# Gate taps of a causal convolution as 64x64 instead of 32x32 array tiles, with weights in plain channel order and new engine orders

## The chip, the cores and the metric

One core of a Trainium2 chip. The metric is the device time of one execution in microseconds, without the host. A profiled execution also gives a span (from the first to the last instruction that counts), which is about 2 us shorter than its time. Medians are given with the number of runs. Every run is put beside runs of the kernel before on the same chip. The sets of experiments ran on different chips (6, then 5, 4 and 0, in the order below), so where kernels of two sets are compared the text says so: such a difference holds that of the chips and sets too (the kernel before had medians of 246.38, 245.32, 247.37 and 245.95 us there).

## The reference, cut to what matters

Feature-map attention (exp of a projection and of its negative, each shifted by its absolute maximum), then a gated linear unit whose gate is a causal convolution over 5 tokens, one weight per channel and tap. Eight batches, 8 heads x 64 channels, 576 tokens.

```python
proj = einsum('bhsd,df->bhsf', x, w_phi)          # q and k
proj = proj - max(abs(proj)); phi = concat(exp(proj), exp(-proj))
kv, z = einsum(k_p, v), sum(k_p);  x = (q_p @ kv) / (q_p @ z + 1e-6)
...
for k in range(5):
    gate_pre += conv_w[k][None, None, :] * xp[:, k:k + S, :]
out = (sigmoid(gate_pre) * (x @ w_val)) @ w_out
```

## The kernel before

Every step is an entry ("op") with a number. Five fixed tables give the order of the entries on TensorE (PE), VectorE (DVE), ScalarE (ACT), GpSimd (POOL) and the load and store queue (SP); a planner walks them, places PSUM banks and sets the semaphore waits. All batches run through one unrolled program, so nothing is a loop on the chip.

Tokens are split by parity: even tokens in partitions 0 to 63 of a head, odd in 64 to 127. The gate is done on TensorE, as a product with diagonal matrices (`DG`), one per tap:

```python
for a in range(2):                     # two halves of the channel tiles
    gps = [Banks(2, "GATE"), Banks(2, "GATE")]
    for y in range(3):
        steps = (((0, 0),), ((0, 1), (2, 0), (2, 1), (4, 0), (4, 1)), ((1, 0), (1, 1), (3, 0), (3, 1)))[y]
        for k, z in steps:             # tap k, half z of the 64 channels
            for g in range(4):
                for par in range(2):
                    p0, dl = D * par + 32 * z, k // 2 + (k & 1) * (1 - par)
                    matmul(PS[32 * g:32 * g + 32, gps[z].at + (par ^ (k & 1)), 0:HALF],
                           DG[p0:p0 + 32, 2 * g + a, k, :], XT[p0:p0 + 32, 2 * g + a, dl:dl + HALF], ...)
        # the third group (odd taps) waits for the end of the second
    ... tanh (ACT), value projection (PE), product (DVE), two channel tiles a half
```

An odd tap takes a token to the other parity, so its result goes to the other parity's bank. The fence, a wait of one gate group for the end of another, keeps the two row halves of the array out of one bank. The 32-channel tiles need the channels of w_val and w_out in another order: four DVE copies (`WVp`) at the start and four transfers for w_out.

## Time and profile before

| | before |
|---|---|
| time, first set | 248.2 us (248.1 to 249.18, 3 runs) |
| profiled execution | 244.11 us, span 242.3 us |
| TensorE records | 4,624 weight loads, as many matmuls |
| gate | 1,280 of these matmuls and 1,280 loads |

The page gives for each engine how much of 40 equal slices it was busy, in tenths; the granted clock of TensorE and the DMA share stand below in the same slices.

```profile
PE   0587588779897997988789959987789999999960
...
PEclk9999997999999999999979999999999999999997
DMA  5999999955589969699996997996744102210361
```

TensorE has dents in the middle (a 5 in slice 24), and none in slices 31 to 38. The clock's dent in slice 21 follows one pause. The instructions of the gate's line, and what the engine idled for ahead of them:

```profile
L881 PEld LDWEIGHTS PS<-XT,DG x1280: 87/88/92, 51.9 to 226.4; 32*32 32x32 bf16 x183
L881 PE MATMUL PS<-XT,DG x1280: 277/289/293, 51.9 to 226.5; 32*32 32x288 bf16 x183
...
  issue: 10.7, 11
  PE PS L881: 3.7, 14
```

(min/median/max ns; then the idle time in us and how often, by what ended it.) "issue" is the largest, and the 3.7 us in 14 times are the fence. Almost two thirds of the idle time ahead of these instructions (10.7 of 16.8 us over all releasers) has no visible cause. The view counts loads and matmuls as two engines, so a pause of both stands in it twice: of the 10.7 us, 4.2 are the matmuls' own, in two pauses.

### The profile page before, as it was taken

How to read it: one execution, taken by the hardware profiler on the slowest of the kernel's cores; microseconds unless marked ns; L12 is line 12 of the kernel's file. 1: busy time of each engine (PE TensorE's matmuls, PEld its weight loads, DVE VectorE, ACT ScalarE, POOL GpSimd, SP SyncE). 2: the span in 40 equal slices, each digit the busy share in tenths (PEclk: the TensorE clock that was granted, in tenths of full speed). 3: DMA queues.
4: the chain of work that ended last, by engine and by line, in shares of the span. 5: the costliest groups of instructions: out<-in, count | busy, mean ns of one | idle time of the engine just before them, and what ended most of it. 6: DMA issues, size and time to landing. Idle time of an engine off the chain costs nothing.

```text
span 242.3 us, 10298 instructions
## 1 busy us (share of the span) xinstructions
PE 197.7 (82%) x4609; PEld 136.8 (56%) x4624; DVE 178.6 (74%) x286; ACT 177.7 (73%) x253; POOL 125.6 (52%) x213
## 2 busy tenths in 40 slices
PE   0587588779897997988789959987789999999960
PEld 0355356656656784655576546664566767775520
DVE  3399978869999996883859549997779877567520
ACT  3278998899899887796927949997859768742220
POOL 7968599792669794338083982670557610000000
PEclk9999997999999999999979999999999999999997
DMA  5999999955589969699996997996744102210361
GB/s 131 208 212 276 206 228 215 222 65 104 131 211 209 227 142 153 128 225 259 173 222 118 187 177 209 201 153 209 213 88 145 49 3 89 98 40 16 119 219 41
DMA packets 59741, 38.30 MB, mean 158 GB/s; under 512 B 37869, under 2 KB 51565, under 8 KB 59634
## 3 DMA queue, kind: packets, MB, share of 16 engines
q1 hardware_dynamic: 48248, 27.67, 48.5%
q0 software_dynamic: 11280, 9.91, 26.9%
q8 instruction: 36, 0.59, 1.0%
q10 hardware_dynamic: 170, 0.08, 0.1%
q14 instruction: 7, 0.06, 0.1%
HBM read 30.48 MB, written 16.52 MB: 194 GB/s over the span
## 4 chain that ended last, share of the span: by engine, by line
PE 61%; DVE 15%; ACT 8%; issue 6%; DMA 5%; POOL 1%; POOLq 0%; DVEq 0%; SPq 0%
PE PS L901 14%; PE PS L930 10%; PE PS L881 8%; PE PS L794 6%; PE PS L756 5%; DVE MQb L674 3%; DMA QT<-R 3%; PE PS L575 3%; ACT KTIL L586 3%; DVE MK L581 2%; DMA KTIL<-in_q_dram 2%; PE PS L661 2%; PE PS L702 2%; DVE XN L808 2%; ACT QTIL L715 2%
## 5 line engine op out<-in xcount | busy, mean ns | idle before, releaser
L623 POOL TENSOR_TENSOR VT<-VN,EK 128x512 bf16<-128x512 f32 x64 | 65.8, 1046 | 29.4 <-ACT EK L614 17.2
L586 ACT ACTIVATE KTIL<-PS 128x1024 bf16<-128x1024 f32 x64 | 63.0, 1045 | 15.2 <-PE PS L575 14.9
L715 ACT ACTIVATE QTIL<-PS 128x1024 bf16<-128x1024 f32 x64 | 62.1, 1048 | 5.1 <-PE PS L708 4.3
L674 DVE TENSOR_REDUCE MQb<-PS 128x8 bf16<-128x1024 f32 (+1 forms) x40 | 43.8, 1112 | 10.0 <-PE PS L661 9.6
L581 DVE TENSOR_REDUCE MK<-PS 128x8 f32<-128x1024 f32 x32 | 38.7, 1217 | 2.3 <-PE PS L575 1.2
L901 PE MATMUL PS<-XT,WV 64*128 64x288 bf16 x512 | 36.1, 283 | 1.3 <-ACT GS L895 0.5
L907 DVE SCALAR_TENSOR_TENSOR GV<-GS,PS 128x576 bf16<-128x576 bf16 x32 | 23.9, 751 | 15.7 <-PE PS L901 11.8
L895 ACT ACTIVATE GS<-PS 128x576 bf16<-128x576 f32 x32 | 19.2, 649 | 18.9 <-PE PS L881 18.9
L930 PE MATMUL PS<-WO,GV 128*128 128x512 bf16 x113 | 28.7, 380 | 1.8 <-issue 1.0
L901 PEld LDWEIGHTS PS<-XT,WV 64*128 64x128 bf16 x512 | 23.3, 94 | 9.4 <-ACT GS L895 1.4
L881 PE MATMUL PS<-XT,DG 32*32 32x288 bf16 x1280 | 20.5, 287 | 6.0 <-issue 4.2
L794 PE MATMUL PS<-KVSB,QTIL 128*128 128x65 bf16 x512 | 21.3, 198 | 3.6 <-issue 3.2
L756 PE MATMUL PS<-VT,KTIL 128*128 128x65 bf16 x512 | 21.0, 196 | 3.0 <-issue 2.4
L794 PEld LDWEIGHTS PS<-KVSB,QTIL 128*128 128x128 bf16 x512 | 18.6, 100 | 7.1 <-issue 3.7
L808 DVE TENSOR_TENSOR XN<-PS,RC 128x512 bf16<-128x512 f32 x32 | 21.9, 689 | 0.9
L552 ACT ACTIVATE OS<-PS 128x512 f32<-128x512 f32 x26 | 15.6, 611 | 9.3 <-PE PS L930 6.2
L756 PEld LDWEIGHTS PS<-VT,KTIL 128*128 128x128 bf16 x512 | 19.0, 99 | 4.8 <-issue 3.4
L633 POOL TENSOR_TENSOR VTt<-VNt,EK 128x512 bf16<-128x512 f32 x16 | 16.6, 1041 | 8.9 <-ACT EK L614 8.8
L611 POOL TENSOR_SCALAR MK<-MK 128x16 f32<-128x16 f32 (+1 forms) x24 | 5.8, 244 | 27.5 <-DVE MK L581 23.0
L881 PEld LDWEIGHTS PS<-XT,DG 32*32 32x32 bf16 x1280 | 10.8, 88 | 14.2 <-issue 6.5
L930 PEld LDWEIGHTS PS<-WO,GV 128*128 128x128 bf16 x128 | 10.7, 98 | 12.0 <-ACT OS L552 0.7
L575 PE MATMUL PS<-W,KT 64*128 64x128 bf16 x256 | 14.0, 242 | 3.4 <-ACT EK L614 0.9
(85 smaller groups left out, 290.4 us busy)
## 6 DMA issues: line engine op xcount, KB each, us to landing
VN<-in_v_dram SPq DMA_DIRECT2D x16, 512.0 KB, 6.3
out_dram<-OS SPq DMA_DIRECT2D x32, 256.0 KB, 3.3
R<-in_k_dram POOLq DMA_DIRECT2D x12, 288.0 KB, 7.0
R<-in_q_dram POOLq DMA_DIRECT2D x12, 288.0 KB, 5.9
QTIL<-in_k_dram SPq DMA_DIRECT2D x2, 512.0 KB, 5.0
VNt<-in_v_dram SPq DMA_DIRECT2D x32, 32.0 KB, 4.6
out_dram<-OS SPq DMA_DIRECT2D x16, 64.0 KB, 2.4
KTIL<-in_q_dram POOLq DMA_DIRECT2D x2, 256.0 KB, 6.0
```

The lines of the kernel that those rows point to most:

```text
L581: pl.op("Kmax", "DVE", dve(1024), lambda E, at, u=u: [E.tensor_reduce(MK[:, 0, 8 * u:8 * u + 8].rearrange("p (t x) -> p t x", t=2), m.PS[: ...
L586: pl.op("Kexp", "ACT", act(1024), lambda E, at, u=u, g=g: [E.activation(KTIL[:, g, u, :, :, :], m.PS[:, at:at + 2, :].rearrange("p t (x f) ...
L623: pl.op("VT", "POOL", pool(512), lambda E, at, u=u, hh=hh, a=a, g=g, EK=EK: [E.tensor_tensor(m.VT[s][:, g, u, :, :, 0:D], m.VN[s][:, 4 * h ...
L674: pl.op("Qmax", "DVE", dve(256 * nx), lambda E, at, u=u, nx=nx: [E.tensor_reduce(MQb[:, :].rearrange("p (t s) -> p t s", t=2)[:, :, 4 * u: ...
L715: pl.op("Qexp", "ACT", act(1024), lambda E, at, u=u, g=g: [E.activation(m.QTIL[s][:, g, u, :, :, :], m.PS[:, at:at + 2, :].rearrange("p t ...
L756: res.append(E.matmul(m.PS[:, at + sg, x * E1:(x + 1) * E1], m.KTIL[s][:, sg, 2 * g + a, par, x, :], m.VT[s][:, sg, 2 * g + a, par, x, :], ...
L794: return [E.matmul(m.PS[:, at + g, x * E1:(x + 1) * E1], m.QTIL[s][:, sg, 2 * j + g, par, x, :], m.KVSB[s][:, g, sg, x, :], start=(sg == 0 ...
L808: pl.op("NRM", "DVE", dve(512), lambda E, at, view=view, RC=RC, XN=XN, par=par: [E.tensor_tensor(XN[:, :, par, :].rearrange("p (g x) d -> ...
L881: res.append(E.matmul(m.PS[32 * g:32 * g + 32, gps[z].at + (par ^ (k & 1)), 0:HALF], m.DG[p0:p0 + 32, 2 * g + a, k, :], XT[p0:p0 + 32, 2 * ...
L901: return [E.matmul(m.PS[:, at + p, 0:HALF], m.WV[ROWS[p], h, P * jt:P * jt + P], XT[ROWS[p], h, PAD:PAD + HALF], start=(h == 0), stop=(h = ...
L907: pl.op("GV", "DVE", dve(576), lambda E, at, jt=jt, GS=GS: [E.scalar_tensor_tensor(out=m.GV[jt][:, s, :, :], in0=GS[:, :, :], scalar=1.0, ...
L930: return [E.matmul(m.PS[:, at, :], m.GV[jt][:, s, p, P * j:P * j + P], m.WO[:, jt, :], start=(jt == 0), stop=(jt == 3)) for jt in range(4)]
```

## The change

Its intent: the same gate with fewer and larger matmuls, 64 channels of one parity by 64 outputs, so 40 per half instead of 80; channels in plain order, so no weight copies; four groups in two phases (even taps, then odd taps), so that a fenced group follows not on the group it waits for but on the one after. All five order tables are new, made with a model that knows about instruction pages and about the delay before loads start.

```diff
-            for y in range(3):
-                steps = (((0, 0),), ((0, 1), (2, 0), ...), ((1, 0), (1, 1), (3, 0), (3, 1)))[y]
+            for n in range(4):
+                y, ks = n % 2, ((0, 2, 4), (1, 3))[n // 2]
                 def mm(E, at, jt=2 * a + y, ks=ks):
+                    for k in ks:
+                        for hh in range(2):
                             for par in range(2):
+                                h, dl = 2 * jt + hh, k // 2 + (k & 1) * (1 - par)
-                                    m.PS[32 * g:32 * g + 32, gps[z].at + (par ^ (k & 1)), 0:HALF],
-                                    m.DG[p0:p0 + 32, 2 * g + a, k, :], XT[p0:p0 + 32, ...],
+                                    m.PS[ROWS[hh], at + (par ^ (k & 1)), 0:HALF], m.DG[ROWS[par], h, k, :],
+                                    XT[ROWS[par], h, dl:dl + HALF], ...
-   sync=gate[-1:] if y == 2 else []          # third group waits for the second
+   sync=gate[-2:-1] if n > 1 else []         # group 3 waits for 1, group 4 for 2
...
-    for jt in range(4):  pl.op("WVp", "DVE", ...)          # four weight copies
-    const("WO", "POOL", 2.2, ... for g in range(4) ...)    # four transfers
+    const("WO", "POOL", 0.8, ... one transfer ...)
-        pl.op("DG", "POOL", pool(5 * 32), ...)
+        pl.op("DG", ("POOL", "DVE"), ... 5 * D ...)
+LAG = dict(xk=1.9, xt=1.9)
 ORDER = dict(PE=..., DVE=..., ACT=..., POOL=..., SP=...)   # all new
 LATE = {...}                                               # release times of loads, all new
```

## The prediction

> **What bounds the kernel now.** I read the page first, then the busy time of each engine in stretches that I chose (the startup, two middle stretches with TensorE stalls and without, the last stretch), then the chain of waits in order of time, then the timeline at the pauses that the chain shows.
>
> ```profile
> span 242.3 us, 10298 instructions
> PE 197.7 (82%) x4609; PEld 136.8 (56%) x4624; DVE 178.6 (74%) x286; ACT 177.7 (73%) x253; POOL 125.6 (52%) x213
> ...
> 12.00:52.00 40.00, 30.69 (x526) 21.67 (x529) 34.98 (x57) 35.00 (x50) 31.80 (x55) 0.96 1.17 216
> 52.00:94.00 42.00, 38.30 (x1048) 27.34 (x1048) 38.28 (x54) 37.60 (x55) 30.28 (x52) 1.00 0.79 163
> 94.00:142.00 48.00, 38.85 (x923) 26.94 (x928) 32.39 (x50) 35.58 (x54) 25.13 (x44) 0.96 0.97 181
> 142.00:189.00 47.00, 41.87 (x1002) 29.52 (x993) 40.36 (x60) 40.64 (x58) 23.66 (x38) 1.00 0.79 177
> 189.00:235.00 46.00, 44.83 (x1111) 29.07 (x1112) 28.77 (x51) 25.14 (x37) 4.38 (x6) 1.00 0.19 66
> ```
>
> Columns of the stretches: length, then busy us of PE, weight loads, DVE, ACT, POOL, then granted clock, DMA share, GB/s. The last 46 us are TensorE alone (44.8 busy, the others under two thirds): it works off what it did not get done earlier. So time that TensorE loses after the startup is paid at the end, nearly one for one. It loses most in 94 to 142: busy 81% against 91% in the stretch before, while DVE (67%) and ACT (74%) are slack. The chain says at what:
>
> ```profile
> 95.55 1.50 issue
> ...
> 108.55 1.62 issue
> ...
> 119.81 2.36 issue
> ...
> 139.14 2.60 issue
> ...
> 174.48 1.74 issue
> ```
>
> "issue" means that nothing visible was awaited. The five are 9.82 us. The timeline around the second, and the instruction queue on the page:
>
> ```profile
> 107.27 1.28 PE L881 MATMUL PS<-XT,DG 32*32 32x288 bf16 x78
> 110.18 0.30 PE L881 MATMUL PS<-XT,DG 32*32 32x288 bf16 x2 [1.62 <-issue]
> ...
> q8 instruction: 36, 0.59, 1.0%
> ```
>
> The pause falls inside one run of equal gate matmuls, two before its end: no data or semaphore explains that. TensorE has about 9,300 records (4,624 loads, as many matmuls, some others), and 9,300/256 = 36.3; the instruction queue moved 36 transfers of 0.59 MB/36 = 16 KB. So TensorE's program comes in pages of 256 instructions, and it stops where the next page is late. In the trace, each pause lies at a page end, and the transfer of the missing page ends about 1.4 us before work resumes. A pause has a second cost:
>
> ```profile
> 121.00:123.20 2.20, 1.03 (x31) 1.03 (x31) 0.00 (x0) 0.60 (x2) 1.32 (x3) 1.00 1.00 211
> 123.20:127.00 3.80, 3.60 (x60) 3.13 (x59) 2.92 (x7) 1.02 (x1) 3.63 (x5) 0.55 1.25 213
> ```
>
> After the 2.36 us pause the granted clock is 0.55 for 3.8 us. By my durations below, the page run then holds 5.5 us of work and took 6.7: about 1.2 us lost.
>
> The startup is another regime: from 12 to 52 us DVE and ACT are 87% busy and lead the chain. Two pieces matter, a wait for the tail of a q tile, and the re-layout of w_val on DVE:
>
> ```profile
> 4.07 5.53 DMA KTIL<-in_q_dram
> ...
> 44.48 1.00 DVE WV L454 x3
> ```
>
> [...] The value projection (16 matmuls, two tiles abreast, 8 rounds) takes 0.99 us on the chain, 0.124 us a round[...]. [...]
>
> **The change part by part.**
> - Gate matmuls. Before: 80 per half batch (8 + 40 + 32), 1,280 in all, 32x32 tiles. On the chain a half is 0.70 + 0.47 to 0.56 us, with the fence about 1.22 us; 1.17/80 = 14.6 ns per matmul with its load[...]. After: 40 per half, four 64x64 tiles abreast[...]. TensorE's time for the gate stays at 16 x 1.22 = 19.5 us. No gain here.
> - The fence. Before, the third group waits for the one just before it (14 waits, 3.7 us of load idle, 0.26 each, already in the 1.22). After, group 3 waits for group 1 while group 2 (0.36 us) runs, so the drain is covered. The first tanh of a half may start 0.24 us sooner. I book 0.
> - Instructions. 640 matmuls and 640 loads go: 9,300 to 8,020, 36 pages to 31.
> - Page density, the main term. I walked both order tables, gave each entry its matmuls and loads, cut at 256 and summed typical durations of the trace before (K 0.38, QA 0.33, QF 0.55, KV 1.3, NUM 0.59, VAL 0.95, OUT 0.86, gate as above). TensorE's sum is 190.5 us in both. Before, 14 of the pages from the first gate on hold under 4.6 us of work (lowest 3.2); after, none does (lowest 4.8, mean about 5.9). The five pauses end pages of 3.97, 4.53, 4.97, 3.73 and 4.52 us; with the pause added, the page turn took 5.5, 6.2, 7.3, 6.3 and 6.3 us. Five such turns against pages of 5.8 us leave 0 + 0.4 + 1.5 + 0.5 + 0.5 = 2.9 us. Gain 9.8 - 2.9 = 6.9 us, and 1.2 us of clock if the long pause goes: 8 us.
> - Weights. Channels in plain order take four DVE copies away (4 x 0.418 = 1.7 us, 1.0 of it on the chain) and one w_out issue replaces four (2.2 to 0.6 us of POOL). The diagonals double to 320 elements: at POOL's slope (1046 - 450)/(512 - 160) = 1.7 ns an element some 0.72 us each instead of 0.45; seven on POOL, one on DVE. POOL comes out even, DVE gains about 1 us at startup.
> - Order of loads. Small q transfers (the tails, which the chain waits for above) now come ahead of the identity on POOL, and the first K work stands behind one q tail, the first that POOL issues, instead of two. That should be some 2 us sooner at 10.7 us, less what the identity loses by coming later. I book 1.5 us of startup.
> - Output copies: 22 on ACT and 14 on DVE instead of 26 and 10: ACT -2.4 us, DVE +2.8. Neither bounds the late part.
> Sum: 6.9 + 1.2 + 1 + 1.5 = 10.6 us at most.
>
> **The rivals.** (a) DVE and ACT take over. Squeezing 8 us out of 94 to 142 would put TensorE at 97%, which no stretch but the last reaches; the stretches around it stop at 89 to 91%. At 91% it would last 38.85/0.91 = 42.7 us, 5.3 less, not 8. So I give back about 2 us. (b) DMA takes over: its share is 0.97 in that stretch and the transposed q of batch 6 was awaited at 157 to 165 on the chain (7.5 us, though TensorE stood only 1.4). The same bytes come in less time, so such waits may grow; the last stretch, with DMA at 0.19, leaves room to absorb it. I give back 1 to 2 us; at worst it eats all but 3 us (245). (c) Streaming binds harder than thought: if four 64-column loads a round do not hide, a half takes 1.6 us, 16 x 0.4 = 6 us back, time about 246 to 247. Against it: 128x64 numerator tiles already do 16 matmuls in 0.37 us. (d) The fetch delay is chance and the page turns stay near 7 us: then pages of 5.9 still pause, and only 4 us are won (244). (e) The new order, being made with a truer model, also removes other TensorE idle time (about 9 us after 52 us that is no page pause): 232 to 235.
>
> **Range and chances.** 10.6 - 3.6 for (a) and (b), plus some 2 for (e): about 9 us off. Time 248.2 - 9 = 239.2, so 239 us. The range 232 to 246 holds (e) below and (b), (c), (d) above. Two per cent is 243.2: I put 0.79 on faster, 0.18 on within, 0.03 on slower, since I see no term that adds more than 6 us against a sure loss of 1,280 instructions.
>
> **What would show it.** Right: 31 transfers on the instruction queue; "issue" pieces over 1 us on the chain two or fewer, under 4 us in sum; gate halves of 1.2 to 1.3 us from 40 matmuls; TensorE near 90% from 94 us on; first gate at about 49 us instead of 51.9; last stretch still TensorE alone. Wrong: pauses of 2 us at page ends as before (d); gate halves of 1.5 us or more (c); TensorE waiting for transposed q or k (b) or for exponentials and maxima (a) where it paused before.

## The result, and the profile after

238.97 us median (238.13 to 240.96, 4 runs) against 248.15 (246.58 to 249.18, 4 runs): faster. The ratio of the fast runs is 0.9647, 95% interval 0.9567 to 0.9727. Ratios are the mean time of one kernel's fast runs over the mean of the other's fast runs of the same rounds, so not quite the ratio of the medians. One caution for what follows. A run counts as slow when it lies more than 1.5% above the fastest of its kernel, and the kernel before scatters from 241 to 252 us in the later sets, so its fast runs are its lucky ones. The changed kernel, run again, then shows a ratio of 0.9836 (0.9722 to 0.9951, by the rule "unclear"), but medians of 239.54 (6 runs) and 245.32 (27 runs), which is 0.976. Where the scatter is wide I compare medians of all runs; the deciding set below gives the fast runs beside them.

The same views of the changed kernel (page; stretches; chain), in the columns named before:

```profile
span 236.1 us, 9023 instructions
PE 203.4 (86%) x3984; PEld 138.3 (59%) x3984; DVE 180.1 (76%) x286; ACT 176.3 (75%) x251; POOL 124.9 (53%) x207
PEclk9999997999999999999999999999999999999997
...
q8 instruction: 31, 0.51, 0.9%
...
12.00:52.00 40.00, 30.75 (x507) 20.97 (x505) 34.04 (x58) 34.71 (x48) 28.11 (x48) 0.96 1.24 212
52.00:94.00 42.00, 38.42 (x823) 25.75 (x819) 37.95 (x53) 37.56 (x55) 29.20 (x49) 1.00 0.70 148
94.00:142.00 48.00, 45.47 (x958) 31.18 (x944) 39.67 (x61) 37.46 (x54) 31.81 (x54) 1.00 1.06 196
142.00:189.00 47.00, 46.27 (x984) 32.29 (x980) 41.03 (x62) 41.14 (x59) 25.74 (x41) 1.00 0.82 178
189.00:229.00 40.00, 39.29 (x709) 25.57 (x701) 24.26 (x45) 21.12 (x31) 0.00 (x0) 1.00 0.23 76
...
124.53 1.66 issue
```

31 transfers of instructions instead of 36; one "issue" piece over 1 us in the chain, 1.66 us, instead of five with 9.8 us; the clock's dent in the middle is gone. TensorE is 95% busy from 94 to 142 (81% before) and 98% from 142 to 189 (89%), and the last stretch, TensorE alone as before, is 6 us shorter. The first 94 us got no better: summing the same typical durations of the entries that TensorE had started by then (an estimate of mine, good to about 1 us) gives 61.8 us of work by 94 us against 64.4 before, then 106.3 against 102.2 by 142 us and 152.0 against 145.6 by 189 us. So the startup and the first batches lost about 2.6 us, and the middle won about 9.

A half of the gate now looks like this in the timeline (start, length, line, tiles, count):

```profile
108.60 1.45 PE L872 MATMUL PS<-XT,DG 64*64 64x288 bf16 x40
109.98 1.16 PE L892 MATMUL PS<-XT,WV 64*128 64x288 bf16 x16
```

From its start to the next group's start it takes 1.38 us, where the half of before takes 1.22 us. In the trace of single matmuls the ten rounds of four start 123 ns apart; the first round takes 147 ns, the round after a fence 144 ns, and the first matmul of the next, 64x128, kind starts 226 ns after the last round, about 100 ns more than a round. The same extra shows at other changes of tile: after a 64x128 matmul of the value projection the next of that tile starts 118 ns later where the work changes, one of the gate 210 ns later, and after a 64x128 matmul of 128 columns it is 52 and 146 ns (92 and 94 ns more).

### The profile page after: what moved, and what is told of

The parts are those of the page before. It is cut to its first block, busy times and chain, and to the rows that moved or that the text cites. A ratio compares the mean times of both kernels' runs of the same rounds, so it can differ in the third digit from the quotient of the medians.

```text
span 236.1 us, 9023 instructions
## 1 busy us (share of the span) xinstructions
PE 203.4 (86%) x3984; PEld 138.3 (59%) x3984; DVE 180.1 (76%) x286; ACT 176.3 (75%) x251; POOL 124.9 (53%) x207
## 4 chain that ended last, share of the span: by engine, by line
PE 62%; DVE 21%; ACT 7%; DMA 3%; issue 2%; POOL 2%; SPq 0%; DVEq 0%; ACTq 0%; POOLq 0%
PE PS L892 13%; PE PS L872 10%; PE PS L921 9%; DVE MK L573 7%; PE PS L748 6%; PE PS L786 5%; DVE MQb L666 4%; ACT KTIL L578 3%; PE PS L694 3%; DMA QTIL<-in_k_dram 3%; PE PS L653 3%; DVE XN L800 3%; PE PS L567 3%; PE PS L700 2%; PE PS L805 2%
## 5 line engine op out<-in xcount | busy, mean ns | idle before, releaser
L578 ACT ACTIVATE KTIL<-PS 128x1024 bf16<-128x1024 f32 x64 | 63.8, 1045 | 8.1 <-PE PS L567 4.3
L921 PE MATMUL PS<-WO,GV 128*128 128x512 bf16 x128 | 32.1, 380 | 0.7 <-DVE MQb L666 0.5
L544 ACT ACTIVATE OS<-PS 128x512 f32<-128x512 f32 x22 | 13.7, 621 | 17.9 <-PE PS L921 14.7
L872 PE MATMUL PS<-XT,DG 64*64 64x288 bf16 x640 | 26.0, 289 | 0.8 <-ACT GS L886 0.4
L886 ACT ACTIVATE GS<-PS 128x576 bf16<-128x576 f32 x32 | 19.7, 652 | 7.5 <-PE PS L872 7.4
L786 PE MATMUL PS<-KVSB,QTIL 128*128 128x65 bf16 x512 | 19.7, 193 | 2.1 <-DVE XN L800 2.1
L786 PEld LDWEIGHTS PS<-KVSB,QTIL 128*128 128x128 bf16 x512 | 17.3, 97 | 6.1 <-DVE XN L800 2.4
L872 PEld LDWEIGHTS PS<-XT,DG 64*64 64x64 bf16 x640 | 14.8, 105 | 8.6 <-issue 1.6
L921 PEld LDWEIGHTS PS<-WO,GV 128*128 128x128 bf16 x128 | 10.6, 98 | 12.0 <-DVE MK L573 0.8
```

The costliest lines, as they stand in the source:

```text
L578: pl.op("Kexp", "ACT", act(1024), lambda E, at, u=u, g=g: [E.activation(KTIL[:, g, u, :, :, :], m.PS[:, at:at + 2, :].rearrange("p t (x f) ...
L786: return [E.matmul(m.PS[:, at + g, x * E1:(x + 1) * E1], m.QTIL[s][:, sg, 2 * j + g, par, x, :], m.KVSB[s][:, g, sg, x, :], start=(sg == 0 ...
L872: res.append(E.matmul(m.PS[ROWS[hh], at + (par ^ (k & 1)), 0:HALF], m.DG[ROWS[par], h, k, :], XT[ROWS[par], h, dl:dl + HALF], start=(k == ...
L921: return [E.matmul(m.PS[:, at, :], m.GV[jt][:, s, p, P * j:P * j + P], m.WO[:, jt, :], start=(jt == 0), stop=(jt == 3)) for jt in range(4)]
```

## The experiments

The question is not whether the time fell but which part did it: the number of TensorE instructions (my theory, by way of late instruction pages), the form of the gate with its fence and plain weights, or the new order. All results were correct.

### Only the instruction count put back, in the new order

Each gate matmul is cut into two of 144 columns. Same order, fences and tiles, but 4,624 matmuls again.

```diff
-    for hh in range(2):
-        for par in range(2):
-            ... m.PS[..., 0:HALF], XT[..., dl:dl + HALF], start=(k == 0)
+    for c in (0, HALF // 2):
+        for hh in range(2):
+            for par in range(2):
+                ... m.PS[..., c:c + HALF // 2], XT[..., dl + c:dl + c + HALF // 2], start=(k == 0 and c == 0)
```

> The changed kernel with each gate matmul cut into two of 144 columns: order, fences, tiles, columns streamed and results as in the changed kernel, but 1,280 gate matmuls and loads again, so 36 instruction pages instead of 31, 10 of them under 4.6 us of work (none in the changed kernel, 14 in the kernel before). Theory (late instruction pages): three to six issue pauses of 1 us or more come back, 5 to 9 us in sum, time 243 to 248 us. Rival (the better order, the covered fence or the plain channels made the gain): one or two pauses, time 238 to 241 us. The gate half must stay at about 1.4 us in the undisturbed halves; if it grows, that part is not the pages.

Measured: 242.68 us median (239.22 to 249.27, 20 runs), just under the lower edge of what the theory gave and above the rival's. It is 3.1 us above the 239.54 of the changed kernel, which ran on another chip, and 2.1 us above it if each median is divided by that of the kernel before in its set (0.985 against 0.976). Its profiled execution was one of the slowest (249.27 us, granted clock 0.975), with page-end pauses of 2.12, 0.89 and 3.62 us. The gate halves are 1.41 us instead of 1.38, half a microsecond in all. So the count costs something by itself in this order, some 2 to 3 us, but less than the change won.

### The old order with the new gates

The order tables of the kernel before, with the third gate entry replaced by groups 3 and 4, and without the entries of the weight copies.

```diff
 ORDER: each (GATE a.0, a.1, a.2) of the old tables -> (a.0), (a.1), (a.2, a.3) of the new groups
+ the 64x64 gates, DG of 64 columns, w_val and w_out in plain order of the change; no LAG
```

> The order tables of the kernel before (each gate entry mapped on the new groups, the third on groups 3 and 4), with the 64x64 gates and plain channels of the change. 31 pages, none under 4.6 us of work. Theory: the pauses go without the new order, at most two over 1 us, time 239 to 243 us. Rival (the new order, from a model with instruction pages, makes the gain): four or more pauses stay, time 245 to 249 us.

Measured: 236.84 us (235.95 to 239.71, 4 runs), below even the theory's range: the new gates in the old order look faster than the whole change. That one ran on other chips; the deciding set below puts the two side by side. Its profiled execution has no page pause over 1 us from the first gate on, and its gate halves are 1.38 us.

### The fence put back in the open

In the 11 halves where groups 1 to 4 stand together, TensorE's order becomes 1, 3, 2, 4.

```diff
-GATE a.0, a.1, a.2, a.3
+GATE a.0, a.2, a.1, a.3      # each fenced group right behind the one it waits for
```

> The changed kernel with gate groups 2 and 3 swapped in the order of TensorE, in the 11 of 16 halves where the four stand together as 1, 2, 3, 4: each fenced group now follows straight on the group that it waits for. If a covered fence is worth what the old fence showed (0.23 us exposed), these halves grow from 1.38 to about 1.8 us (two exposed fences), 11 x 0.45 = 5 us, time about 243 us. If fences cost nothing, 239 us.

Measured: 242.56 us (240.13 to 247.66, 20 runs), as expected if fences cost. The half of the gate in its timeline, with the start of what follows:

```profile
218.44 1.96 PE L915 MATMUL PS<-XT,DG 64*64 64x288 bf16 x40
220.33 1.90 PE L935 MATMUL PS<-XT,WV 64*128 64x288 bf16 x28
```

1.89 us instead of 1.38, 0.25 us a fence. Eleven halves make 5.6 us on TensorE, of which 2 to 3 us show in the time (3.0 against the 239.54 of another chip, 2.0 with each median divided by that of its kernel before). The two-phase order with a covered fence is what keeps the 64x64 half within 0.16 us of the 32x32 one.

### The new order with the old gates

> The order tables of the change with the 32x32 gates and the weight copies of the kernel before. 36 pages, 10 under 4.6 us of work. Theory: pauses of 5 to 9 us in sum, time 244 to 249 us, as before or nearly. Rival (order alone): at most two pauses, time 238 to 241 us.

This one could not be scheduled: in the new order some halves have group 3 ahead of group 2, and the old third group waits for the second. Mended, with the old groups kept in sequence:

```diff
 ORDER: (a.0), (a.1), (a.2) of the new tables -> the old three groups, the second never behind the third
+ four weight copies on DVE where the new order had a diagonal product
```

> The new order with the 32x32 gates and the weight copies of the kernel before; the third gate group stands right after the second where the new order had its groups apart. 36 pages, 11 under 4.6 us of work. Theory: pauses of 5 to 9 us in sum, 245 to 250 us, no better than the kernel before. Rival (the order makes the gain): 238 to 241 us.

Measured: 250.84 us (247.23 to 254.6, 6 runs) beside 245.32 for the kernel before in that set: the order alone wins nothing, it loses. The weight copies were placed by me, and the first gate came at 56.6 us, so the 5.5 us are not the order's alone and this is no clean test of it. Page pauses in its profile: 1.97, 1.30 and 0.87 us.

### The deciding set: both kernels' parts side by side

> The changed kernel itself again, as the reference of this set. Expected 238 to 241 us, with zero to two issue pauses over 1 us.

> The old order with the new gates again, beside the changed kernel on the same chip. If the new order is worth nothing by itself or costs time in the startup (its work at 94 us was 1.4 us behind in the first look), this stays at 236 to 238 us, one or two us below the changed kernel. If the first look was luck, 239 to 241 us.

> The old order with the new gates, each gate matmul cut into two of 144 columns: against the run before it only the number of TensorE instructions changes (8,000 to 9,300, pages 31 to 36, pages under 4.6 us of work 0 to 11). Theory (late pages): 243 to 247 us, pauses of 5 to 9 us in sum. Rival (the form of the gate, its fence or the plain weights made the gain, not the count): 237 to 239 us.

The third of these is the second plus the cut into 144 columns shown above, so between the two only the number of instructions changes. Medians of the set:

| kernel | TensorE pages | median us | runs | mean of fast runs | ratio of fast runs, 95% |
|---|---|---|---|---|---|
| before (old order, 32x32 gates) | 36 | 245.32 | 27 | 243.54 (11) | |
| old order, 64x64 gates, matmuls cut in two | 36 | 245.08 | 22 | 243.04 (11) | 0.9983 (0.9941 to 1.0025) |
| old order, 64x64 gates | 31 | 236.60 | 6 | 236.58 (5) | 0.9745 (0.9641 to 0.9849) |
| the change (new order, 64x64 gates) | 31 | 239.54 | 6 | 239.05 (5) | 0.9836 (0.9722 to 0.9951) |
| new order, 32x32 gates | 36 | 250.84 | 6 | 249.15 (4) | 1.0263 (1.0117 to 1.0409) |

Read from the top: larger tiles, plain weights and covered fence without fewer instructions are worth 0.2 us; fewer instructions alone 8.5 us; the new order costs 2.9 us. By the fast runs alone these are 0.5, 6.5 and 2.5 us, and the change won 4.5 us instead of 5.8. The rival "form" falls, as a net gain, with the second row, the rival "order" with the fourth and fifth. The timelines of TensorE in the second and third rows at the same gate, first with the cut:

```profile
135.78 0.41 PE L920 MATMUL PS<-XT,DG 64*64 64x144 bf16 x11
138.62 1.37 PE L920 MATMUL PS<-XT,DG 64*64 64x144 bf16 x47 [2.44 <-issue]
```

```profile
134.87 1.45 PE L919 MATMUL PS<-XT,DG 64*64 64x288 bf16 x40
136.25 0.40 PE L700 MATMUL PS<-W,QT 64*128 64x128 bf16 x8
136.48 0.78 PE L939 MATMUL PS<-XT,WV 64*128 64x288 bf16 x9
138.76 0.66 PE L939 MATMUL PS<-XT,WV 64*128 64x288 bf16 x7 [1.50 <-issue]
```

The pause again falls inside a run of equal matmuls, in the middle of the gate with the cut; without it the page reaches further, and the pause comes later and is shorter. That such pauses are page ends can be counted: in the nine traces where no matmul record is missing, TensorE stopped 12 times for 1 us or more between 52 and 225 us. The nine stops for which the profile shows no releaser all come at record 193 plus a multiple of 256 (counted from 0), the three that have one (1.27, 2.79 and 7.23 us) at none. The page-end pauses of the two profiled executions (from the first gate on) are 1.17 + 2.44 + 0.87 = 4.5 us and 1.5 us, their times 244.01 and 238.58 us. Of these 5.4 us the pauses make 3.0 and the gate halves 0.5. For the other 1.9 us the traces show two candidates, whose shares were not measured: page-end pauses of 0.2 to 0.7 us (1.8 us in sum with the cut, 0.5 without), and a half-clock stretch of 3.41 us right after the pause of 2.44 us, worth up to 1.7 us, which the kernel without the cut does not have. One profile is one draw from a scatter of several us.

### Is it DMA that makes a page late?

Twelve more cast transfers are issued by POOL after its last work, so DMA is busy in the last stretch, where it was idle; nothing waits for them but the end of the program. Once with the kernel before, once with the old order and the new gates.

```diff
+for n in range(12):
+    pl.op("extra", "POOL", ..., dma_start(X[n], (k, q)[n % 2][2 + n // 4][...]))   # unused DRAM
```

> The kernel before with 12 more cast transfers (k and q of late batches, 288 KB each, into unused DRAM), issued by POOL after its last work, so DMA is busy from about 190 to 215 us where it was at 0.2. No engine waits for them but the end. Theory (an instruction page comes late when DMA is busy): in that stretch the page transfers start later after the page turn (they start within 0.6 us there now, up to 4.6 us in the busy middle), and TensorE, with pages of 3.2 to 4.8 us of work there, gets two or more new pauses of 1 us or more, 3 to 8 us longer in all. Rival (the pauses belong to the program, not to DMA): no new pause, 0 to 1 us longer.

> The old order with the new gates, with the same 12 extra transfers after the last work of POOL. Theory: the page transfers start as late as in the run before, but the pages there hold 5.2 to 8 us of work, so at most one new pause of 1 us, 0 to 3 us longer than without them (236.6 us). Rival as above: 0 to 1 us longer.

Measured: 251.73 us (248.29 to 255.07, 4 runs) beside 247.37 (11 runs) for the kernel before, 4.4 us more (7.0 by the fast runs, but these are two of each); and 237.33 us (4 runs) for the new gates, 0.7 more than without, though that was on another chip. The stretch 189 to 215 us of the kernel before, then of the kernel before with the transfers, with its two stretches after that:

```profile
189.00:215.00 26.00, 25.73 (x739) 17.95 (x740) 17.36 (x31) 17.64 (x26) 4.38 (x6) 1.00 0.16 54
```

```profile
189.00:215.00 26.00, 25.73 (x701) 18.41 (x704) 18.17 (x33) 18.95 (x27) 11.54 (x22) 1.00 0.79 166
215.00:218.50 3.50, 1.49 (x76) 0.78 (x73) 1.02 (x2) 0.13 (x1) 0.00 (x0) 0.97 1.09 261
218.50:222.00 3.50, 3.50 (x40) 2.45 (x38) 0.76 (x1) 3.00 (x4) 0.00 (x0) 0.55 0.41 105
...
214.66 0.43 PE L930 MATMUL PS<-XT,DG 32*32 32x288 bf16 x21
217.09 0.45 PE L930 MATMUL PS<-XT,DG 32*32 32x288 bf16 x27 [2.01 <-issue]
```

DMA share goes from 0.16 to 0.79. The transfers on the instruction queue can be set against the point at which TensorE enters a new page (every 256 of its records in the trace, with the offset taken from where the pauses fall). They start there about 2.5 to 3.7 us after it, where they started 0 to 1.2 us after it without the extra load. The old gates get a pause of 2.01 us inside a gate group and 3.5 us at a clock of 0.55 behind it. I expected two pauses and saw one; the last wait for the transfers lengthened the end by about 1 us too, so not all of the 4.4 us is the page. With the new gates the transfers start as late (2.4 to 3.2 us) and there is no pause: their pages hold 5.2 to 8 us of work, more than the delay. So, by one profile of each, DMA load makes a page late, and the work in a page decides whether it is felt.

### What does the new order lose?

Three tries, none of which found it; all ran on other chips than the 239.54 us of the changed kernel, so a difference of 1 us could not be seen. First the one diagonal product that the new order put on DVE. It took more than I had booked; the timeline of DVE in the changed kernel:

```profile
46.15 1.29 DVE L443 TENSOR_TENSOR DG<-I,CWT 128x320 bf16<-128x320 bf16 x1
```

```diff
-DVE: ... Qmax, DG 3, Qmax ...
+POOL: DG 3 behind the other seven
```

> The changed kernel with the one diagonal product that the new order put on DVE (1.29 us, 1.21 us of it on the chain at 46 us) moved to POOL behind the other seven. If it is what the new order loses in the startup, first gate at about 52 instead of 53 us and 238 to 238.5 us, one us below the changed kernel. If not, 239 to 240 us.

Measured: 239.14 us (237.37 to 241.16, 6 runs), 0.4 below the changed kernel and within its scatter; the first gate came at 52.4 us. At most a small part.

Then the gate groups that the new order spreads:

```diff
 six halves of the 16: GATE a.0 ... a.2 ... a.1 ... a.3  ->  a.0, a.1, a.2, a.3 at the place of the first
```

> The changed kernel with the four gate groups of a half one after the other in the 6 of 16 halves where the new order had other work between them. Each separate piece pays a mode change (about 0.1 us of drain each way by the trace, up to three pieces a half, so 6 halves x 3 x 0.2 us = 2 to 3.5 us at most). If that is what the new order loses against the old order with new gates, 236.5 to 238 us. If not, 239 to 240 us, or more where the PSUM banks are then short.

Measured: 240.92 us (238.17 to 243.65, 6 runs): no better, rather worse. And the order of loads and stores:

```diff
-SP order and LATE of the change
+SP order and LATE of the kernel before        # the other four engines as in the change
```

> The changed kernel with the order of the load and store queue (SP) and the release times of the loads taken from the kernel before; TensorE, DVE, ACT and POOL keep the new order. In the changed kernel DMA is busy 0.57 to 0.59 of the stretch 52 to 75 us against 0.75 to 0.77 in the old order with new gates, so its loads are let go later. If that is what the new order loses, 236.5 to 238 us. If the loss is in the compute order, 239 to 240 us or more (loads that now come at times which the order doesn't want).

Measured: 258.03 us (256.31 to 259.49, 6 runs). TensorE waits 7.2 us once for values of a batch whose loads now come out of step with POOL's order. This shows that the five tables are fitted to each other, not that the loads of the change are good or bad. Two other mixes (new order for compute with old order for POOL and loads, and the reverse) could not be scheduled at all. Where the 2.9 us go stays open. The progress sums say when: in the first look the old order with new gates is about 1.4 us of work ahead of the changed kernel at 94 us and 2.8 at 189 us; in the deciding set about 3.2 and 1.3 us, where the changed kernel had a page pause of 2.15 us at 83 us.

The fastest version found is therefore the old order with the new gates: 236.60 us, below both kernels.

## Why the prediction was right or wrong

The time (239 us predicted, 238.97 measured) was right, and so was the main term, the pages. That it was right to the microsecond is luck: the gate and the startup were booked too well, the order has the wrong sign, 3.6 us given back to rivals were not taken there, and in the first set the kernel before had slower runs than later. Side by side the change won 5.8 us (4.5 by the fast runs), not 9.

- Pages, 6.9 + 1.2 us: right. In the first profile the chain's pauses fell from 9.8 to 1.66 us, 8.2 us less where 6.9 was booked, and the clock's dent in the middle went. 31 transfers, one pause over 1 us, TensorE above 90% after 94 us: all as foreseen. The count alone is worth 8.5 us in the old order (236.60 against 245.08); in the new order the cut gives back only 2 to 3, so its size depends on the order; that this is by where the page ends fall was not tested.
- Gate time "stays", 0 us: wrong by one term. I took ten bare rounds for the new half, by estimate (the value projection's 0.99 us for 8 rounds is 0.124 us a round), but a measured interval, which holds the extra 0.10 us before the first matmul of another tile, for the old one. The new half takes 1.38, 0.16 more: about 0.10 for that extra and 0.05 for the first round (147 ns) and the round behind the fence (144 ns). 16 x 0.16 = 2.6 us.
- Fence booked as 0: it does cost next to nothing as built (the round behind it starts after 144 ns instead of 123). Uncovered it costs 0.25 us each, so without the two-phase order the gate would have been 16 x 0.51 = 8 us longer on TensorE.
- Startup, 1 + 1.5 us: wrong. The first gate came at 52.8 us, not at about 49 (51.9 before); the first K work at 10.2 us instead of 10.7. The product on DVE took 1.29 us, for which I had only POOL's slope. But the old order without the copies has its first gate at 53.2 and 53.8 us and the same kernel with cut matmuls at 51.6, so single executions differ there by 2 us and the removed copies are not seen at all.
- Rival (a), DVE and ACT as a ceiling near 91%: wrong. TensorE reached 95 and 98% in the middle. Rival (b), waits for DMA taking over: in the first profile TensorE's waits for transposed data no longer show among its longest. So the 3.6 us that I gave back were not taken there. (Of them 2 were for (a); its own figures, 8 - 5.3, give 2.7.)
- Point (e), the new order as a gain of about 2 us: wrong in sign, it costs 2.9 us.
- Rival (c): the four tiles do run abreast, 123 ns a round; its 1.6 us a half was an estimate of mine without a measurement under it. Rival (d): mostly not, but not never. Of the four profiles of the changed kernel and of the old order with the new gates, one has no page pause of 1 us; the others have one each, of 1.66, 2.14 and 1.50 us, behind pages that held 5.7, 5.7 and 6.0 us of work.

In sum: I booked 10.6 - 3.6 + 2 = 9.0 us. What the runs show is 8.5 from the count, nearly nothing from the form, and 2.9 lost by the order, 5.8 us where all five stood side by side (6.5, 0.5 and 2.5, so 4.5, by the fast runs), and 9.2 us in the first set, where the kernel before had slower runs. The gain of the count is shown by the cut; that it comes by way of the pages is shown for 3.0 of 5.4 us in one pair of profiles.

## What to carry to other kernels

In a long unrolled program, count instructions as a cost of their own: here TensorE stopped for 1.5 to 2.6 us at the ends of pages of 256 while DMA was busy (a share of 0.97 and 0.79 in the stretches that hold the five pauses). This hit pages of 3.7 to 5.0 us of work often (five in the kernel before), and pages of 5.7 to 6.0 us in three of four profiles with the new gates, once in each. Look for idle time with no releaser inside a run of equal instructions, and prefer fewer, larger instructions to a finer tiling that is no faster. Take a change apart before keeping all of it: here one part won 8.5 us (6.5 by the fast runs) and another gave back 2.9 (2.5).

## What the traces show of pages, tiles, fences and the clock

- Pages. At the turns of most of the 36 pages of 256 records TensorE of the kernel before stopped for less than 1 us, but at five of them for 9.8 us of a 242 us span. The runs show two conditions: DMA load (transfers start about 2.5 to 3.7 us after the page turn instead of 0 to 1.2) and little work in the page (the five pauses came behind 3.7 to 5.0 us of work).
- Page transfers. One took 0.9 to 1.3 us mostly, and work resumed about 1.4 us after its end (1.3 to 1.6 in the kernel before). There are 36 turns of a page and 36 transfers of 16 KB, and each of the five pauses ended behind a transfer that had started only 2.9 to 5.5 us after the turn before it.
- Tiles. The first matmul of another tile comes about 100 ns late here, and the finer tiling multiplies the program: 32x32 and 64x64 gates take 1.22 and 1.38 us a half, yet in the old order the kernel with the finer ones is 8.7 us slower, all but 0.2 of it by the count.
- Fences. One that follows right on its group costs 0.25 us, next to nothing (144 ns instead of 123 for a round) with 0.36 us of other work between.
- Clock. The granted clock of TensorE changes in steps of 3.413 us (in the kernel before 3.413 us at half clock, then 81.92 us at full, 3.413 at half, 112.64 at full). I cut the 14 traces into stretches of that length, counted from each trace's first drop, from about 41 us to 225 us. All ten in which TensorE was idle for 2.0 us or more were followed by one at half clock; after those with less this was so three times (1.29, 1.38 and 1.69 us). So in these traces it mattered how a pause fell: those of 2.36 and 2.01 us lay in one stretch (2.34 and 2.01 us of it) and were followed by 3.41 us at half clock, the one of 2.60 us was divided over two (1.17 and 1.43 us) and was not.
